# A fused attention and MLP kernel: doubles made float32 by one 16-bit conversion and one join, the MLP of the first 256 tokens in float32

## The chip, the cores and the metric

One core of a Trainium2 chip runs the whole kernel. The metric is device time in microseconds, the median of three runs. Engines are called PE (matrix multiply, its weight loads PEld), DVE (vector), ACT (scalar), POOL and SP; SP issues all copies between HBM and on-chip memory.

## The reference

```python
def _attn_ref(q, k, v):                      # (4, 8, 576, 64) float32
...
    q_rot, k_rot = (rotate(q), rotate(k))
    scale = 1.0 / np.sqrt(D)
    scores = scale * np.matmul(q_rot, k_rot.transpose(0, 1, 3, 2))
    scores = scores - np.max(scores, axis=-1, keepdims=True)
    attn = np.exp(scores)
    attn = attn / (np.sum(attn, axis=-1, keepdims=True) + 1e-09)
    return np.matmul(attn, v).astype(np.float32)
...
def _moe_ref(x, w_in, w_out):                # x (2304, 512), w_in (512, 2048), w_out (2048, 512)
    h = x @ w_in
...
    g = np.where(pos, h, np.where(neg, 0.0, (h + beta) ** 2 / (4.0 * beta)))
    return (g @ w_out).astype(np.float32)
```

`rotate` is the rotary turn of the two halves of a head by cos and sin. The two weight matrices arrive as doubles (8 bytes an element, 8.4 MB each); everything else is float32. The accuracy asked for is that of float32.

## The kernel before

**Numbers in halves.** PE multiplies float16 faster than float32, so most operands are split into a high and a low float16 half (`high` writes hi = x times a factor, `split` then lo = x times the factor minus hi), and a product is three matmuls: hi·hi, hi·lo, lo·hi (`TERMS`). For sample 0 the scores are float32 matmuls (L562), since its k and q are used before their factors are known.

**Stages.** Four samples of 576 queries, each in blocks of two 128-query tiles; the last 64 queries of two samples are packed together ("left"). For a tile and a pair of heads: scores (L564, or L562 in float32), maximum (L534, DVE), exponential with sum (L536, ACT), sum scaled (L539) and inverted (L541), the probabilities split into halves (L314 or L316 and L545), both halves transposed by a DMA through SP (L243), values (L612, 14 float16 matmuls a head), out of PSUM as halves (L623, L626). Then the MLP of a block: `psH` = x·w_in (L720), the piecewise square in four or five elementwise steps (L732 to L748, its low half at L748), `psO` = g·w_out (L757), out (L770). Block 0 (sample 0, queries 0 to 255) runs its MLP as two units of 128 tokens (`SPLIT`); all later blocks take 256 tokens at a time, so their L720 matmuls have 256 columns. The first of those begins block 1 of sample 0.

**Weights.** `prep_w` runs 16 times (8 pieces each of w_in and w_out): a copy of 1 MB of doubles, three DVE integer operations that pack sign, exponent and mantissa into float32 (L493, L495, L497), the high half (L314, ACT), and the low half by PE and ACT in `rest`: per third of a piece a float32 matmul with the identity (L430) and a bfloat16 one with the negated diagonal (L431) add up y - hi in PSUM, and ACT writes it out (L434).

**Order.** Nothing is scheduled at run time. Every step is added to a plan with an engine; `ORDER`, a list of numbers written into the file, says in which order they are issued, and `ON_VECTOR` which engine takes a step that ACT or DVE could do. Each engine works through its list in order and waits at a step whose inputs are not there.

Of the kernel before, what the change touches and what calls it, by code (L numbers as in the profile page):

```python
# [923 lines left out]
```

## Time and profile before

| | us |
|---|---|
| median of 3 runs (lowest, highest) | 604.23 (603.35, 605.54) |
| the profiled execution, its own time | 603.99 |
| its span, from first to last instruction | 602.2 |
| PE busy | 575.7 (96%) |
| DVE busy | 508.8 (84%) |
| ACT busy | 418.5 (70%) |

Busy time is the union of an engine's instructions; consecutive instructions of DVE and ACT overlap by some hundredths of a microsecond, so the step from one start to the next is a little shorter than the duration given for one. A float32 matmul appears in the trace as two records. The span is cut below at 167.1 us, where the first 256-column matmul starts.

### The profile page before, as it was taken

To read this page: it belongs to the slowest core of one execution; us is meant where nothing else is said; L and a number is where in the kernel's file an instruction comes from. 1 tells how busy PE (TensorE), PEld (TensorE's weight loads), DVE (VectorE), ACT (ScalarE), POOL (GpSimd) and SP (SyncE) were. 2 spreads that over 40 slices of the span, in tenths; PEclk is the share of its full clock that TensorE was granted. 3 is DMA by queue.
4 is the path that set the end of the run, shared out by engine and by line. 5 is a ranking of instruction groups with operands and counts; after the bars stand their busy time and mean duration, and the time that the engine had idled before them with its cause. 6 is when DMAs were issued, how large, how long until landed. Compare 5 with 4: busy or idle time off the path is not lost.

```text
span 602.2 us, 12605 instructions
## 1 busy us (share of the span) xinstructions
PE 575.7 (96%) x5074; PEld 378.4 (63%) x5074; DVE 508.8 (84%) x823; ACT 418.5 (70%) x849; POOL 0.7 (0%) x6
## 2 busy tenths in 40 slices
...
GB/s 310 384 209 248 280 271 264 263 194 160 240 173 201 206 115 79 195 118 138 221 187 118 85 149 152 72 105 107 103 79 97 119 114 80 112 60 1 2 36 19
DMA packets 182571, 91.34 MB, mean 152 GB/s; under 512 B 170608, under 2 KB 171888, under 8 KB 180464
## 3 DMA queue, kind: packets, MB, share of 16 engines
...
q8 instruction: 40, 0.66, 0.4%
...
## 4 chain that ended last, share of the span: by engine, by line
PE 75%; DVE 14%; ACT 5%; DMA 3%; issue 2%; SPq 0%; DVEq 0%; ACTq 0%
PE psH L720 29%; PE psO L757 27%; PE psV L612 7%; PE psS L564 6%; DVE phl L545 3%; PE psS L430 3%; DVE sca L534 3%; DMA pT<-phl 2%; DMA w<-in_w_in_dram 1%; PE psS L562 1%; ACT p L536 1%; DVE dup L287 1%; ACT phl L314 1%; ACT w L434 1%; PE psS L590 1%
## 5 line engine op out<-in xcount | busy, mean ns | idle before, releaser
L720 PE MATMUL psH<-xT,w 128*128 128x256 f16 (+1 forms) x2112 | 206.4, 253 | 0.2
L757 PE MATMUL psO<-w,g 128*128 128x512 f16 x864 | 202.0, 379 | 0.2 <-DVE g L748 0.2
L720 PEld LDWEIGHTS <-w 128*128 128x128 f16 x2112 | 174.4, 98 | 31.3 <-issue 2.5
L536 ACT ACTIVATE p<-psS,sca 128x576 f32<-128x576 f32 x144 | 105.8, 736 | 63.2 <-DVE sca L534 41.2
L757 PEld LDWEIGHTS <-g 128*128 128x128 f16 x864 | 82.1, 98 | 85.5 <-issue 2.6
L545 DVE SCALAR_TENSOR_TENSOR phl<-p,sca,phl 128x576 f16<-128x576 f32 x144 | 115.8, 811 | 4.7 <-ACT phl L314 3.8
L534 DVE TENSOR_REDUCE sca<-psS 128x1 f32<-128x576 f32 x144 | 105.5, 749 | 4.9 <-PE psS L564 3.2
L314 ACT ACTIVATE phl<-p,sca 128x576 f16<-128x576 f32 x97 | 72.8, 767 | 12.8 <-DVE sca L541 10.2
L737 ACT ACTIVATE a<-psH 128x512 f32<-128x512 f32 x72 | 42.6, 591 | 47.1 <-PE psH L720 44.3
L740 DVE SCALAR_TENSOR_TENSOR r<-a,r 128x512 f32<-128x512 f32 x72 | 49.3, 685 | 25.0 <-ACT r L735 24.5
L748 DVE SCALAR_TENSOR_TENSOR g<-r,g 128x512 f16<-128x512 f32 x72 | 49.5, 688 | 12.1 <-ACT g L743 10.1
L612 PE MATMUL psV<-pT,vS 128*64 128x320 f16 (+2 forms) x576 | 43.8, 275 | 2.2 <-DVE phl L545 1.7
L564 PE MATMUL psS<-kT,qT 64*128 64x64 f16 (+1 forms) x576 | 44.1, 284 | 1.3 <-ACT p L536 1.3
L564 PEld LDWEIGHTS <-qT 64*128 64x128 f16 x576 | 23.0, 94 | 30.6 <-issue 13.6
L734 ACT ACTIVATE r<-a 128x512 f32<-128x512 f32 x48 | 30.1, 627 | 8.4 <-DVE g L748 6.7
L612 PEld LDWEIGHTS <-vS 128*64 128x64 f16 x576 | 27.8, 109 | 10.7 <-issue 7.4
L743 ACT ACTIVATE g<-r 128x512 f16<-128x512 f32 x40 | 24.9, 622 | 10.4 <-DVE r L740 10.3
L735 ACT ACTIVATE r<-r 128x512 f32<-128x512 f32 x48 | 30.2, 630 | 1.5
L434 ACT ACTIVATE w<-psS,sca 128x341 f16<-128x341 f32 (+1 forms) x48 | 25.5, 538 | 6.1 <-PE psS L562 3.0
L536 ACT ACTIVATION_READ_ACCUMULATOR p<-psS,sca 128x1 f32 x144 | 28.2, 196 | 0.0
L316 DVE TENSOR_SCALAR phl<-p,sca 128x576 f16<-128x576 f32 x47 | 24.2, 516 | 2.1 <-DMA pT<-phl 1.3
L732 DVE SCALAR_TENSOR_TENSOR r<-a 128x512 f32<-128x512 f32 x24 | 16.5, 689 | 11.0 <-ACT a L737 10.6
...
## 6 DMA issues: line engine op xcount, KB each, us to landing
...
```

The source lines that it names most:

```text
L314: plan.add("act", act_cost(n), at, lambda: nc.scalar.activation(out=hi, in_=x, func=AF.Copy, scale=f), r=r, w=w)
L434: plan.add("act", act_cost(cut.stop - cut.start, psum=True), at, lambda cut=cut, bank=bank: nc.scalar.activation(out=lo[:, cut], in_=bank, ...
L534: plan.add("dve", dve_cost(S, psum=True), at, lambda m=m, src=src: nc.vector.tensor_reduce(out=m, in_=src, op=ALU.max, axis=AX.X, negate=T ...
L536: plan.add("act", act_cost(S, psum=True, ptrs=2), at, lambda a=a, e=e, m=m, src=src: nc.scalar.activation(out=p32[e], in_=src, func=AF.Exp ...
L545: plan.add("dve", dve_cost(S, ptrs=1), at, lambda a=a, e=e, hi=hi, lo=lo: nc.vector.scalar_tensor_tensor(out=lo, in0=p32[e], scalar=rr[:, ...
L564: nc.tensor.matmul(out=psS[a][:, lo:hi], lhsT=qT[hf][d, l, j, c:c + 128], rhs=kT[ks][d, j, m, lo:hi], start=z == 0, stop=z == 2)
L612: nc.tensor.matmul(out=outs[a], lhsT=st, rhs=moving(a, blk), start=z == 0, stop=z == len(seq) - 1)
L720: nc.tensor.matmul(out=psH[:, n * i:n * i + n], lhsT=wi[ft // 2][:, wl, kk, 128 * (ft % 2):128 * (ft % 2) + 128], rhs=xfn(xl, kk), start=z ...
L737: plan.add("act", act_cost(512, psum=True, ptrs=0), at, lambda one=one: nc.scalar.activation(out=a, in_=psH, func=AF.Relu, scale=2.0 ** -7 ...
L740: plan.add("dve", dve_cost(512), at, lambda one=one: nc.vector.scalar_tensor_tensor(out=r, in0=a, scalar=one, in1=r, op0=ALU.max, op1=ALU. ...
L748: plan.add("dve", dve_cost(512), at, lambda g=g, one=one: nc.vector.scalar_tensor_tensor(out=g[:, 1], in0=r, scalar=-one, in1=g[:, 0], op0 ...
L757: nc.tensor.matmul(out=psO[pos[tt]], lhsT=g[:, gl, n * i + 128 * tt:n * i + 128 * tt + 128], rhs=wo[ft // 2][:, wl, ft % 2, :], start=ft = ...
```

## The change

It does the following.

- **Doubles.** A piece is copied from its second 16-bit word on (`raw[:, 0:4095]` from `[:, 1:4096]`), so that the top 16 bits and the middle 32 bits of each double are aligned. One conversion bfloat16 to float16 of the top words (L519 on ACT, 13 times; L521 on DVE, 3 times) drops exponent bits; one DVE shift-and-or (L522) joins it with the middle words to float32. The conversions all write one buffer, `top`.
- **Weights stay float32 first.** `full(i)` holds piece i in float32 in the place of the halves of piece i + 1. `halve_w` makes the halves later, between the units of block 0 (`SEQ`, each `C` four pieces): high as before, low by DVE alone (L540). `rest` is not called any more (`PE_LO` is empty).
- **MLP of block 0** (256 tokens) in float32 matmuls (L857, L894): no halves of x or g.
- **Values of the first 128 queries** in float32 (`item32`): PE transposes the probabilities by matmuls with a diagonal of 1/sum (L626, L638), ACT or DVE takes them out of PSUM, and PE multiplies them with v as loaded (L648, L652). The DMA transposes and halves of that tile are gone.
- **Sample 0's k and first q** are loaded once; the exchanged half is made by a matmul with a signed permutation (`nrl`, L321) in the place of the second identity matmul.
- Sample 3 has more softmax buffers; the last output is taken out in two halves, on both engines where `ON_VECTOR` says so; `ORDER` and `ON_VECTOR` are new.

```diff
--- before.py
+++ after.py
...
 ORDER = """
-1 0 1 0 7 74 6 11 10 16 1 21 0 87 40 5 0 1 63 11 0 14 1 59 25 1 0 2 29 1 21 0 248 9 13 4 48 0 243 47 11 242 1 26
...
+2 1 1 0 11 34 45 22 17 6 0 118 117 0 41 8 0 38 7 26 37 54 1 25 64 0 28 1 18 8 0 0 9 0 8 1 4 0 93 94 94 95 94 92
...
-PE_TILES = 16
-PE_SUMS = 4
-PE_Q1 = 0
-SPLIT = {0:"aabbabab"}
-PE_V = 0
+PE_LO = ()
+ATT32 = (0,)
+WHOLE = (0, 1)
+SEQ = "aabCbCabCabC"
+WIDE = 8
+PE_Q1 = False
+SPLIT = (0,)
...
+    xF = [x0[:, 1024 * z:1024 * z + 1024].bitcast(F32).rearrange("p (k n) -> p k n", k=KT) for z in range(2)]
+    xb = x0[:, 1024:2048].rearrange("p (l k n) -> p l k n", l=2, k=KT)
     idn = k1[:, 0:256].bitcast(F32)
+    nrl = x1[:, 2048:2304].bitcast(F32)
...
+                def both(bank=bank, cut=cut, j=j):
+                    nc.tensor.matmul(out=bank[:, 0:m], lhsT=idn, rhs=x[:, j, cut], start=True, stop=False)
+                    nc.tensor.matmul(out=bank[:, 0:m], lhsT=nrl, rhs=y[:, j, cut], start=False, stop=True)
+
...
+    top, tk = k1_[:, 0:2048], ["top"]
+    spare = k1_[:, 2048:4096].bitcast(F32)
...
+    def full(i):
+
+        if i == 2 * NW - 1:
+            return spare, ["spare"]
+        return ws[:, i + 1].rearrange("p l f -> p (l f)").bitcast(F32), [("w", l, i + 1) for l in range(2)]
...
-        dma(at, raw, (w_out if which else w_in).bitcast(U32)[c], [], rk_, 128 * 8192)
+        dma(at, raw[:, 0:4095], (w_out if which else w_in).bitcast(U16)[c][:, 1:4096], [], rk_, 128 * 8192)
...
+        head = raw.bitcast(BF16)[:, 2::4]
+        middle = raw.bitcast(U32)[:, 0::2]
+        cast = top.bitcast(F16)[:, 1::2]
+        if plan.pick() == "act":
+            plan.add("act", act_cost(1024, ptrs=0), at, lambda: nc.scalar.activation(out=cast, in_=head, func=AF.Copy), r=rk_, w=tk)
+        else:
+            plan.add("dve", 602.0, at, lambda: nc.vector.tensor_copy(out=cast, in_=head), r=rk_, w=tk)
         plan.add("dve", 1135.0, at, lambda: nc.vector.scalar_tensor_tensor(
-            out=u, in0=lw, scalar=29, in1=u, op0=ALU.logical_shift_right, op1=ALU.bitwise_or), r=rk_ + yk, w=yk)
-        plan.add("dve", 1135.0, at, lambda: nc.vector.scalar_tensor_tensor(
-            out=u, in0=hw, scalar=0xC0000000, in1=u, op0=ALU.bitwise_and, op1=ALU.bitwise_or), r=rk_ + yk, w=yk)
+            out=y.bitcast(U32), in0=middle, scalar=13, in1=top.bitcast(U32), op0=ALU.logical_shift_right, op1=ALU.bitwise_or),
...
+    def halve_w(i, at):
+        c, which = i // 2, i % 2
+        plan.group, plan.part = "wh", i
         f, fk = wcol[which][1]
-        high(at, hi, y, f, 1024, yk + [fk], [("w", 0, i)] + (firstkeys if i in range(4, 8) else []))
-        if c == 0:
+        y, yk = full(i)
+        hi, lo = [ws[:, i, l] for l in range(2)]
+        high(at, hi, y, f, 1024, yk + [fk], [("w", 0, i), ("w", 1, i)])
+        if i not in PE_LO:
+            plan.add("dve", dve_cost(1024, ptrs=1), at, lambda: nc.vector.scalar_tensor_tensor(
+                out=lo, in0=y, scalar=f, in1=hi, op0=ALU.mult, op1=ALU.subtract),
+                r=yk + [fk, ("w", 0, i)], w=[("w", 1, i)])
+            return
...
+    def item32(at, b, t, j, i, c0):
+
+        plan.group, plan.part = "s0", f"{b}{t}{j}"
+        scores(at, b, t, j)
+        s, ri = ring("phl", 2), ring("sums", 4)
...
+            evacuate(at, dg, idn, rr[:, a:a + 1], 128, ["idn", ("sums", ri, 2)], [("dg", d)], fast=True)
+        pt = phl[s].bitcast(F32)
...
+            def turned(src=src, dg=dg, bk=bk):
+                for z in range(4):
+                    nc.tensor.matmul(out=psO[bk][:, 128 * z:128 * z + 128], lhsT=src[:, 128 * z:128 * z + 128], rhs=dg, start=True, stop=True)
+
...
+        def sums_of_values():
+            for z in range(T):
+                for a in range(2):
+                    h = 2 * j + a
+                    nc.tensor.matmul(out=psV[64 * a:64 * a + 64, c0:c0 + 128], lhsT=rv[:, z, D * h:D * h + D],
+                                     rhs=pt[:, 512 * a + 128 * z:512 * a + 128 * z + 128], start=z == 0, stop=False)
+            for a in range(2):
+                h = 2 * j + a
+                nc.tensor.matmul(out=psV[64 * a:64 * a + 64, c0:c0 + 128], lhsT=rvL[64 * a:64 * a + 64, D * h:D * h + D],
+                                 rhs=pt[64 * a:64 * a + 64, 1024:1152], start=False, stop=True)
+
...
 
-                plan.add("pe", pe_cost(12, n), at, mm, r=xkeys + [("w", l, 2 * (ft // 2)) for l in range(2)] + [("w", 1, 2 * (ft // 2), e) for e in range(2)], w=["psH"],
+                if x32 is not None:
+                    def mmf(i=i, ft=ft):
+                        w = full(2 * (ft // 2))[0].rearrange("p (k f) -> p k f", k=KT)
+                        for kk in range(KT):
+                            nc.tensor.matmul(out=psH[:, n * i:n * i + n], lhsT=w[:, kk, 128 * (ft % 2):128 * (ft % 2) + 128],
+                                             rhs=x32[:, kk, :], start=kk == 0, stop=kk == KT - 1)
...
+                        w = full(2 * (ft // 2) + 1)[0].rearrange("p (k f) -> p k f", f=DM)
+                        nc.tensor.matmul(out=psO[pos[0]], lhsT=g32[:, n * i:n * i + 128], rhs=w[:, ft % 2, :],
+                                         start=ft == 0, stop=ft == FT - 1)
+
+                    plan.add("pe", 863.0, at + 0.3, mm2f, r=gkeys + full(2 * (ft // 2) + 1)[1], w=[("psO", pos[0])])
...
         if i in SPLIT:
-            units = [mlp_units(tokens(z, 128), [("xT", int(last), l, j, z) for l in range(2) for j in range(NP)], 128, ats[4 * z:4 * z + 4],
-                               lambda tt, z=z: main_rows(b, ts)(z)) for z in range(2)]
-            for z in SPLIT[i]:
-                next(units["ab".index(z)], None)
+            units = [mlp_units(lambda l, kk: xb[:, l, kk, :], [("xT", 0, l, j, z) for l in range(2) for j in range(NP)], 128, ats[4 * z:4 * z + 4],
+                               lambda tt, z=z: main_rows(b, ts)(z), xF[z] if z in WHOLE else None) for z in range(2)]
+            parts = iter(range(0, 2 * NW, 4))
+            for z in SEQ:
+                if z == "C":
+                    p = next(parts)
+                    for h in range(p, p + 4):
+                        halve_w(h, at)
+                else:
```

**The weights on DVE.** In the list of DVE before, the first pieces of weights stand among the rotary products (L287) and the maxima (L534) of sample 0, three operations a piece; `w` is the raw piece, `xT_77` and `o` are where the float32 goes:

```order
L497 SCALAR_TENSOR_TENSOR xT_77<-w,xT_77 128x1024
L534 TENSOR_REDUCE sca<-psS_92 128x1
L534 TENSOR_REDUCE sca<-psS_93 128x1
L287 TENSOR_TENSOR w<-w,rt 128x256
L493 TENSOR_SCALAR o<-w 128x1024
L287 TENSOR_TENSOR rk<-rk,rt 128x576
L495 SCALAR_TENSOR_TENSOR o<-w,o 128x1024
L287 TENSOR_TENSOR rk<-rk,rt 128x576
L541 RECIPROCAL sca<-sca 128x2
L497 SCALAR_TENSOR_TENSOR o<-w,o 128x1024
```

The same place in the list of DVE of the change; `kT_63` is the buffer `top`:

```order
L584 TENSOR_SCALAR sca<-sca 128x2
L521 CAST kT_63<-w 128x1024
L586 RECIPROCAL sca<-sca 128x2
L522 SCALAR_TENSOR_TENSOR w<-w,kT_63 128x1024
L575 TENSOR_REDUCE sca<-psS_92 128x1
L575 TENSOR_REDUCE sca<-psS_93 128x1
L298 TENSOR_TENSOR w<-rq_85,rt 128x256
L522 SCALAR_TENSOR_TENSOR w<-w,kT_63 128x1024
L293 TENSOR_TENSOR rq_85<-rq_85,rt 128x256
```

One conversion and one join stand for three operations, and the second join's conversion is on ACT's list; the first conversion stands as the 27th instruction of DVE, where L493 was the 10th.

**PE after the first scores.** Before, PE makes low halves of weights between the float32 scores of sample 0 (`psS` is the PSUM of the scores, of which `rest` uses the spare end):

```order
L430 MATMUL psS_93<-xT_77,kT_63 128x341
L431 LDWEIGHTS kT_63
L431 MATMUL psS_93<-w,kT_63 128x341
L430 MATMUL psS_92<-xT_77,kT_63 128x341
L431 LDWEIGHTS kT_63
L431 MATMUL psS_92<-w,kT_63 128x341
L255 MATMUL psS_93<-sca 128x3
L430 MATMUL psS_92<-xT_77,kT_63 128x342
L431 LDWEIGHTS kT_63
L431 MATMUL psS_92<-w,kT_63 128x342
L562 MATMUL psS_92<-kT_62,qT_64 128x512
L562 MATMUL psS_93<-kT_62,qT_64 128x512
```

After, the same stretch of PE's list holds the turning of probabilities of the first tile (`p`) into `psO` and `psH`, and the rotary sums (L320, L321):

```order
L670 MATMUL psS_92<-kT_62,qT_64 128x64
L670 MATMUL psS_93<-kT_62,qT_64 128x64
L638 MATMUL psH<-xT_77,p_0_69 64x128
L638 MATMUL psH<-xT_77,p_1_70 64x128
L626 MATMUL psO_96<-xT_77,p_0_69 128x128 x4
L320 MATMUL psS_93<-rk,kT_63 128x288
L321 MATMUL psS_93<-w,xT_77 128x288
L626 MATMUL psO_97<-xT_77,p_1_70 128x128 x4
L320 MATMUL psS_92<-rq_85,kT_63 128x256
```

All 48 pairs L430 and L431 are gone from PE; four matmuls of 128 columns a head for the transposed probabilities are new.

**DVE ahead of the first 256-column matmul.** Before, the list of DVE up to the last output of attention that this matmul reads (L626 with 320 columns) holds 238 instructions and ends so:

```order
L534 TENSOR_REDUCE sca<-psS_93 128x1
L534 TENSOR_REDUCE sca<-psS_92 128x1
L260 TENSOR_REDUCE sca<-psS_92 128x1
L626 SCALAR_TENSOR_TENSOR xT_77<-psV,sca,xT_77 128x320
L287 TENSOR_TENSOR dup_87<-dup_87,rt 128x1152
L545 SCALAR_TENSOR_TENSOR phl_72<-p_0_69,sca,phl_72 128x576
L324 SCALAR_TENSOR_TENSOR qT_65<-rq_86,sca,qT_65 128x1280
L626 SCALAR_TENSOR_TENSOR xT_77<-psV,sca,xT_77 128x320
```

After, it holds 212 up to the same output (L734) and ends with the last low halves of weights:

```order
L540 SCALAR_TENSOR_TENSOR w<-w,sca 128x1024
L345 SCALAR_TENSOR_TENSOR qT_64<-rq_85,sca,qT_64 128x1024
L734 SCALAR_TENSOR_TENSOR xT_77<-psV,sca,xT_77 128x320
L540 SCALAR_TENSOR_TENSOR w<-w,sca 128x1024
L345 SCALAR_TENSOR_TENSOR qT_65<-rq_86,sca,qT_65 128x1280
L540 SCALAR_TENSOR_TENSOR w<-kT_63,sca,w 128x1024
L278 TENSOR_SCALAR sca<-sca 128x1
L266 TENSOR_REDUCE sca<-psS_92 128x1
L734 SCALAR_TENSOR_TENSOR xT_77<-psV,sca,xT_77 128x320
```

The first scores and the splitting of k of sample 1, which stood ahead of this point, stand behind it now.

## Rows read from the trace of the kernel before

**Rows 1.** Windows: length, busy time of each engine, granted PE clock, DMA share, GB/s.

```profile
core 0: us, PE busy (x) PEld busy (x) DVE busy (x) ACT busy (x) POOL busy (x), PEclk, DMA share, GB/s
0.00:10.50 10.50, 2.81 (x6) 2.12 (x7) 2.43 (x10) 1.69 (x2) 0.70 (x6) 1.00 0.78 266
10.50:32.40 21.90, 17.77 (x72) 10.54 (x72) 21.69 (x40) 15.93 (x40) 0.00 (x0) 1.00 1.05 371
32.40:39.30 6.90, 6.39 (x15) 2.93 (x16) 6.39 (x17) 5.54 (x11) 0.00 (x0) 0.51 0.90 149
39.30:167.10 127.80, 119.03 (x1113) 75.65 (x1109) 124.99 (x174) 117.21 (x232) 0.00 (x0) 1.00 0.98 243
167.10:225.00 57.90, 57.58 (x531) 39.14 (x526) 57.04 (x92) 50.10 (x101) 0.00 (x0) 1.00 0.76 173
225.00:597.60 372.60, 372.13 (x3349) 247.99 (x3347) 296.25 (x495) 227.38 (x465) 0.00 (x0) 1.00 0.53 102
```

**Rows 2.** Timeline: the first 256-column matmul (PE), and the last output (ACT).

```profile
167.12 1.16 PE L720 MATMUL psH<-xT,w 128*128 128x256 f16 x9
...
597.62 0.69 ACT L770 ACTIVATE o<-psO,sca 128x512 f32<-128x512 f32 x1 [5.83 <-PE psO L757]
```

**Rows 3.** Waits of DVE on copies: total us, times, longest.

```profile
DVE w L287 <- DMA w<-in_km_dram: 4.0, 1, 4.0
...
DVE xT L493 <- DMA w<-in_w_in_dram: 2.0, 1, 2.0
```

**Rows 4.** Timeline of DVE: start, duration, instruction.

```profile
10.46 0.69 DVE L493 TENSOR_SCALAR xT<-w 128x1024 uint32<-128x1024 uint32 x1 [2.04 <-DMA w<-in_w_in_dram]
11.07 0.42 DVE L287 TENSOR_TENSOR rq<-rq,rt 128x256 f32<-128x256 f32 x1
11.41 1.22 DVE L495 SCALAR_TENSOR_TENSOR xT<-w,xT 128x1024 uint32<-128x1024 uint32 x1
12.54 0.75 DVE L287 TENSOR_TENSOR w<-w,rt 128x576 f32<-128x576 f32 x1
...
27.58 0.80 DVE L545 SCALAR_TENSOR_TENSOR phl<-p,sca,phl 128x576 f16<-128x576 f32 x1
28.30 0.75 DVE L534 TENSOR_REDUCE sca<-psS 128x1 f32<-128x576 f32 x1
28.96 1.54 DVE L545 SCALAR_TENSOR_TENSOR phl<-p,sca,phl 128x576 f16<-128x576 f32 x2
...
37.10 1.27 DVE L324 SCALAR_TENSOR_TENSOR vS<-rv,sca,vS 128x1024 f16<-128x1024 f32 x1
38.29 0.15 DVE L265 RECIPROCAL sca<-sca 128x1 f32<-128x1 f32 x1
```

**Rows 5.** Groups by form: busy us and mean ns of one, then idle before.

```profile
L748 DVE SCALAR_TENSOR_TENSOR g<-r,g 128x512 f16<-128x512 f32 x72 | 49.5, 688 | 12.1 <-ACT g L743 10.1
...
L434 ACT ACTIVATE w<-psS,sca 128x341 f16<-128x341 f32 x32 | 16.9, 539 | 1.9 <-PE psS L562 1.2 <-PE psS L431 0.5
...
L314 ACT ACTIVATE w<-xT,sca 128x1024 f16<-128x1024 f32 x8 | 9.1, 1138 | 0.3
...
L324 DVE SCALAR_TENSOR_TENSOR kT<-rk,sca,kT 128x1152 f16<-128x1152 f32 x6 | 8.4, 1406 | 0.0
...
L626 DVE SCALAR_TENSOR_TENSOR xT<-psV,sca,xT 128x256 f16<-128x256 f32 x4 | 1.9, 466 | 0.0
```

**Rows 6.** Timeline of PE: float32 sums of 288 columns, then one L430 and L431 pair.

```profile
19.87 0.65 PE L306 MATMUL psS<-w,kT 128*128 128x288 f32 x2
20.36 0.68 PE L305 MATMUL psS<-rk,kT 128*128 128x288 f32 x2
...
98.85 0.79 PE L430 MATMUL psS<-xT,kT 128*128 128x341 f32 x2
99.48 0.31 PE L431 MATMUL psS<-w,kT 128*128 128x341 f16 x1
99.70 1.50 PE L720 MATMUL psH<-xT,w 128*128 128x128 f16 x24
101.03 0.79 PE L430 MATMUL psS<-xT,kT 128*128 128x341 f32 x2
```

**Rows 7.** Timeline of PE's weight loads: float32, one matmul of 3 columns between.

```profile
29.67 0.30 PEld L255 LDWEIGHTS psS<-sca 128*128 128x128 f32 x2 [0.88 <-ACT qT L309]
29.89 0.30 PEld L305 LDWEIGHTS psS<-rk,kT 128*128 128x128 f32 x2
```

More of the change, by code (lines that the diff above doesn't have):

```diff
@@ L14 @@
 U32 = mybir.dt.uint32
+U16 = mybir.dt.uint16
 AF = mybir.ActivationFunctionType
@@ L380, in split_k @@
         hi, lo = [kT[s][:, js[0]:js[0] + n, l, :] for l in range(2)]
-        split(at, hi, [("kT", s, j, 0) for j in js], lo, [("kT", s, j, 1) for j in js] + (["idn", ("ndg", 0), ("ndg", 1)] if b == 1 and 3 in js else []),
-              rk[:, js[0]:js[0] + n, :], [("rk", j) for j in js], kfac[b, js[0]], n * S)
+        gone = (["top", "spare"] + (["idn", ("ndg", 0), ("ndg", 1)] if 3 in js else [])) if b == 1 else []
+        split(at, hi, [("kT", s, j, 0) for j in js], lo, [("kT", s, j, 1) for j in js],
+              rk[:, js[0]:js[0] + n, :], [("rk", j) for j in js], kfac[b, js[0]], n * S, gone=gone)
     def load_q(b, hf, js, at, i):
@@ L481, in prep_w @@
+    made = []
     def prep_w(which, c, at):
-        yi, i = ring("ybufs", 2), 2 * c + which
-        (raw, rk_), y, yk = rawseq[i], ybufs[yi], ykeys[yi]
+        i = 2 * c + which
+        (raw, rk_), (y, yk) = rawseq[i], full(i)
         plan.group, plan.part = "raw w", c
-        dma(at, raw, (w_out if which else w_in).bitcast(U32)[c], [], rk_, 128 * 8192)
+        dma(at, raw[:, 0:4095], (w_out if which else w_in).bitcast(U16)[c][:, 1:4096], [], rk_, 128 * 8192)
         plan.group = "w"
-        words = raw.rearrange("p (n t) -> p n t", t=2)
@@ L489, in prep_w @@
[L489 to L494 removed]
+        head = raw.bitcast(BF16)[:, 2::4]
+        middle = raw.bitcast(U32)[:, 0::2]
+        cast = top.bitcast(F16)[:, 1::2]
+        if plan.pick() == "act":
+            plan.add("act", act_cost(1024, ptrs=0), at, lambda: nc.scalar.activation(out=cast, in_=head, func=AF.Copy), r=rk_, w=tk)
+        else:
+            plan.add("dve", 602.0, at, lambda: nc.vector.tensor_copy(out=cast, in_=head), r=rk_, w=tk)
@@ L499, in prep_w @@
+            r=rk_ + tk, w=yk + (firstkeys if i in range(3, 7) else []))
         if c == 0:
@@ L529, in softmax_item, with exponentials @@
+    begun = set()
+    def exponentials(b, at, nh, ri):
+        many = b == B - 1
         sm, rr = sums[ri][:, 0:nh], sums[ri][:, 2:2 + nh]
         sk = [("sums", ri, a) for a in range(nh)]
-        es = [ring("p32", 3) for _ in range(nh)]
+        es = [ring("end_p32", 5) if many else ring("p32", 3) for _ in range(nh)]
         for a, e in enumerate(es):
-            m, src = mx[ri][a], psS[slot + a][:, 0:S]
+            m, src = mx[ri][a], psS[a][:, 0:S]
             plan.add("dve", dve_cost(S, psum=True), at, lambda m=m, src=src: nc.vector.tensor_reduce(
-                out=m, in_=src, op=ALU.max, axis=AX.X, negate=True), r=[("psS", slot + a)], w=[("mx", ri, a)])
+                out=m, in_=src, op=ALU.max, axis=AX.X, negate=True), r=[("psS", a)], w=[("mx", ri, a)])
@@ L542, in softmax_item @@
+        return es, rr
+    def softmax_item(b, at, nh):
+        many = b == B - 1
+        s, ri = (ring("end_phl", 4) if many else ring("phl", 2)), ring("sums", 4)
+        halves, hk = end_phl[s]
+        own = [z for z in hk if z[0] == "rk" and s not in begun]
+        begun.add(s)
+        es, rr = exponentials(b, at, nh, ri)
         for a, e in enumerate(es):
-            hi, lo = [phl[s][:, S * (2 * a + l):S * (2 * a + l + 1)] for l in range(2)]
-            high(at, hi, p32[e], rr[:, a:a + 1], S, [("p32", e), ("sums", ri, 2)], [("phl", s, 0, a)])
+            hi, lo = [halves[:, S * (2 * a + l):S * (2 * a + l + 1)] for l in range(2)]
+            high(at, hi, end_p32[e][0], rr[:, a:a + 1], S, [*end_p32[e][1], ("sums", ri, 2)], [("phl", s, 0, a)] + (own if a == 0 else []))
@@ L641, in attention_block @@
             for i, t in enumerate(ts):
+                if i == 1:
+                    for c in range(NW - 2, NW):
+                        for which in range(2):
+                            prep_w(which, c, -8.5 + 1.2 * c)
                 w = 128 + (SL if i == left else 0)
@@ L672, in attention_block @@
                 x_out(at - 1, b, [xT[1][:, l, j, x:x + n] for l in range(2)],
-                      [[("xT", 1, l, j, i) for i in range(2)] + [("xL", l, e, j)] for l in range(2)], n)
+                      [[("xT", 1, l, j, i) for i in range(2)] + [("xL", l, e, j)] + ([("dg", d) for d in range(4)] if b == 0 and l == 0 else [])
+                       for l in range(2)], n)
                 continue
@@ L691, in item, with wkeys, mlp_block, mlp_units @@
         scores(at, b, t, j)
-        s = softmax_item(at, 2)
-        dmaT(at, pT[slot][:, :, col:col + 128], phl[s],
+        s = softmax_item(b, at, 2)
+        dmaT(at, pT[slot][:, :, col:col + 128], end_phl[s][0],
              [("phl", s, l, a) for l in range(2) for a in range(2)], [("pT", slot, i)], 128 * 4608)
+    def wkeys(i, half=None):
+        if half == 0 and 0 < i < WIDE:
+            return [("w", 0, i), ("w", 1, i, 0)]
+        return [("w", 0, i), ("w", 1, i)] + [("w", 1, i, e) for e in range(2)]
     nblk = [0]
-    def mlp_block(xfn, xkeys, n, ats, rows):
-        for _ in mlp_units(xfn, xkeys, n, ats, rows):
+    def mlp_block(xfn, xkeys, n, ats, rows, end=False):
+        for _ in mlp_units(xfn, xkeys, n, ats, rows, end=end):
             pass
-    def mlp_units(xfn, xkeys, n, ats, rows):
+    def mlp_units(xfn, xkeys, n, ats, rows, x32=None, end=False):
         nt = n // 128
@@ L767, in mlp_units @@
             oi = ring("o", 2)
-            f, fk = ofac[0]
-            plan.add("act", act_cost(512, psum=True), at + 0.4, lambda tt=tt, oi=oi: nc.scalar.activation(
-                out=o_s[oi], in_=psO[pos[tt]], func=AF.Copy, scale=f), r=[("psO", pos[tt]), fk], w=[("o", oi)])
+            f, fk = (1.0, "ones") if x32 is not None else ofac[0]
+            for e in range(1 + end):
+                cut = slice(0, 512) if not end else slice(256 * e, 256 * e + 256)
+                evacuate(at + 0.4, o_s[oi][:, cut], psO[pos[tt]][:, cut], f, 512 // (1 + end), [("psO", pos[tt]), fk],
+                         [("o", oi, 1) if e else ("o", oi)], 0 if x32 is not None else 1)
             for sl, dst in rows(tt):
-                dma(at + 0.5, dst, o_s[oi][sl], [("o", oi)], [("out", id(dst))], 128 * 2048 // len(rows(tt)))
+                dma(at + 0.5, dst, o_s[oi] if sl is None else o_s[oi][sl], [("o", oi)] + [("o", oi, 1)] * end, [("out", id(dst))], 128 * 2048 // len(rows(tt)))
     def main_rows(b, ts):
@@ L778, in left_rows @@
     def left_rows(b0):
-        return lambda i: [(slice(64 * e, 64 * e + 64), out[(b0 + e) * S + SM:(b0 + e + 1) * S, :]) for e in range(2)]
-    dma(-20, rt, rot, [], ["rt"], 128 * 2 * 4 * S)
+        return lambda i: [(None, out[b0 * S:(b0 + 2) * S, :].rearrange("(e r) c -> e r c", e=2)[:, SM:S, :])]
+    for e, cut in enumerate((slice(0, 256), slice(256, S))):
+        dma(-20, rt[:, :, cut], rot[:, :, cut], [], [("rt", e)], 128 * 8 * (cut.stop - cut.start))
     def init():
         make_identity(nc, idn)
+        i4, r4 = [m.rearrange("p (a b c) -> p a b c", b=2, c=32) for m in (idn, nrl)]
+        for e in range(2):
+            nc.vector.tensor_scalar(out=r4[:, :, e], in0=i4[:, :, 1 - e], scalar1=-1.0, scalar2=None, op0=ALU.mult)
+        nc.vector.memset(top.bitcast(F32), 0.0)
         nc.vector.memset(ones, 1.0)
@@ L790, in init @@
         nc.vector.memset(vZ[64:128], 0.0)
-    plan.add("dve", 1400.0, -20, init, w=["idn", "ones", "vZ", ("ssw", 2), ("ssw", 5)] + [("ssk", i) for i in range(NP)] + [("ssv", i) for i in range(3)])
+    plan.add("dve", 2000.0, -20, init, w=["idn", "top", "spare", ("xL", 1, 0, 1), "ones", "vZ", ("ssw", 2), ("ssw", 5)] + [("ssk", i) for i in range(NP)] + [("ssv", i) for i in range(3)])
     blocks = [(b, ts, i == 1) for b in range(B) for i, ts in enumerate(([0, 1], [2, 3]))]
@@ L815 @@
     prep_v(0, -8)
-    for c in range(NW):
+    for c in range(NW - 2):
         for which in range(2):
```

206 lines of the change are left out of this document (131 added, 75 removed), and 105 rows, old and new, of the table ORDER.

## The prediction

> **What bounds the kernel now.** I read the windows first. From 167.10 us to 597.60 PE is busy 57.58 + 372.13 of 430.5 us: there the time is PE's work and nothing else [rows 1]. Ahead of that it is not. PE is busy 17.77 of 21.9 us, 6.39 of 6.9 and 119.03 of 127.8, while DVE is busy 21.69, 6.39 and 124.99: from 10.5 to 167.1 us DVE stands still for only 3.5 us, PE for 13.4 [rows 1]. So I cut the run at the timeline's first 256-column matmul, at 167.12 us [rows 2]: DVE's list ahead of it decides when it comes, and the matmuls behind it take what they take. The output follows the last matmul by some 5 us [rows 2].
>
> Behind the cut PE's work is nearly the same in both programs. Counted in the two lists: 1,344 matmuls of 256 and 384 of 128 columns into `psH`, and the same values; 780 of 512 columns into `psO` become 768, and 36 score matmuls of sample 1 (18 of 512, 18 of 64 columns, two side by side) move in. At 0.43 ns a column (24 of 128 columns in 1.33 us [rows 6]) that is -2.6 and +2.2 us: it cancels. So the change is worth what it takes off DVE's list ahead of the cut, as long as PE, ACT and the copies follow, and as long as DVE keeps up behind it.
>
> **The change part by part, on DVE ahead of the cut.** Prices are steps from start to start, since durations overlap by some 0.08 us: L493 0.61, L495 1.13 (L497 alike), L545 0.72, L534 0.66, a low half of 1,024 columns (L324) 1.19 [rows 4]. For the others I take the group's mean less 0.08: L748 0.60, L324 of 1,152 columns 1.33, L626 of 256 columns 0.39 [rows 5]. The counts come from the two lists, 238 instructions before and 212 after.
>
> - *Weights.* Out go 16 x (0.61 + 1.13 + 1.13) = 45.9. In come 16 joins (L522) at L495's 1.13 (the same shift-and-or, raw words read at the same spacing) = 18.1; 16 low halves that PE and ACT made before (L540), 16 x 1.19 = 19.0; 3 conversions (L521); one high half more, 0.7; the two diagonals for `rest` go, -0.4. No row shows a 16-bit conversion on DVE: it lies between L493's 0.61 and L495's 1.13, both of 1,024 columns. I take 0.61, since it has one operand like L493; 1.8, or 3.4. Net -6.7 (-5.1).
> - *First tile in float32.* L545 falls from 37 to 28, L534 from 40 to 36, two high halves come in (1.0): -6.5 - 2.7 + 1.0 = -8.2. Of these, the four L534 and one L545 belong to sample 1 and are only moved behind the cut.
> - *MLP of 256 tokens.* L748 falls from 7 to 0, one step of the square more (0.6): -3.6. Four L626 go: -1.6.
> - *Moved.* Two splits of sample 1's k (L324) and one rotary product (L287, 1.27): -3.9.
> - *Added small things.* Three outputs from PSUM, seven scaled sums, the sign matrix: +1.5.
>
> The sum is -22.5 us, of which some 8 are moved rather than saved (3.9 here, 3.4 above, and small ones).
>
> **What is given back, and what else moves.** Behind the cut, from 167.1 to 225.0, DVE is already busy 57.04 of 57.9 us [rows 1]. The moved 8 us land there. From the cut to the start of the next 256-token MLP, DVE's list holds four maxima, two splits of k, one rotary product and one low half more (+7.3), and three rotary products of the next q fewer (two of 1,280, one of 1,024 columns, at L495's step by their width, -3.9): +3.4. If DVE sets the pace to that point, this is lost; if PE does, nothing. I take 3. Behind 225 us DVE is busy 296.25 of 372.6 [rows 1], and nothing more is lost.
>
> The start gains. Of the first 10.5 us DVE works 2.43 [rows 1], for it waits 4.0 us for the first k and 2.0 for the first weights [rows 3]. After, the second copies of sample 0's k and q are not loaded and the first conversion stands 27th instead of 10th, so the second wait goes and the first shortens by one 0.3 MB copy: -3.
>
> The first tile has a longer chain, from 1/sum through diagonals, PE, PSUM and back, instead of halves and a DMA transpose; queued behind each step on PE are scores whose maxima DVE needs next. PE's list of the change puts rotary sums between the steps. I take +2 for stalls, from 0 to 8 (twice the largest wait that DVE has on a copy now [rows 3]).
>
> *PE ahead of the cut* must not become the bound. Out go 48 pairs L430 and L431 at 0.85 (98.85 to 99.70) [rows 6]: -41. For float32 the two records of 288 columns take 0.49 [rows 6], so 0.85 ns a column and record, 1.7 a column. The MLP's 128 matmuls of 128 columns and 32 of 512 come to 27.9 + 27.9, against 384 float16 ones at 0.055 (24 in 1.33 us [rows 6]) and 96 at 0.22: 55.8 - 42.2 = +13.6. The first tile: 32 transposes of 128 columns at 0.22, 48 half-width matmuls at 0.11, less 112 float16 half-width ones at 0.028: +9. Together -18. PE's 146 busy us ahead of the cut become 128; with the 8 before its first matmul 136, of the 145 that DVE leaves: it follows, with 9 us of room against 13 before.
>
> *ACT* loses 48 evacuations L434 at 0.46 (mean less 0.08 [rows 5]), 22, and gains 13 conversions. No row shows one; a float32 to float16 copy of the same 1,024 columns takes 1.14 [rows 5], the nearest, and I take 1.06 with overlap: 13.8. ACT was busy 140 of 167 us and becomes 130 or so of 145: hidden.
>
> *Copies.* Four large transposes and eight small loads go. The 16 weight copies now start 2 bytes into their rows; no row shows such a start. I take their time as unchanged.
>
> *End.* The last output takes ACT 0.69 [rows 2]; in two halves on two engines, -0.3.
>
> Sum: -22.5 + 3 - 3 + 2 - 0.3 = -20.8. From the span of 602.2 that is 581.4. The profiled execution lasted 603.99, 1.8 beside its span, and the median of the runs is 604.23, 0.2 above it. So 583.4, say **583.5 us**.
>
> **The rivals.** *Conversion in place of integers as a new wait.* The buffer `top` is single: a conversion on ACT waits for the join of the piece before on DVE, and the next join waits for the conversion. Queued behind a join on DVE are the maxima and low halves that PE waits for. If each of the 13 pairs costs DVE 1.06 us, 14 us of the gain go: 597. For it: ACT is busy 92% of 39.3 to 167.1 [rows 1]. Against it: joins stand several instructions behind one another in the list, and half of them at least find the conversion done: 590 to 597.
>
> *Float32 weight loads show.* A float32 matmul loads its weights once a record, and two loads with next to no matmul between take 0.22 us (29.67 to 29.89 [rows 7]), 0.11 each. Behind 240 ns of columns that is hidden [rows 6]; 128 columns stream for 0.11 too, just as long. If load and stream did not overlap, the MLP's 128 and the tile's 32 matmuls of 128 columns would pay 2 x 0.11 each, 35 us; PE's 136 ahead of the cut become 171, the cut comes there and not at 145: 609 at the most, a little slower than now. I give it little, as loads run under the stream in every row shown; a quarter of it would leave the forecast, since PE has 9 us of room. The Trainium skill, TensorE: Matmul & The Clock Gate, section "LDWEIGHTS (loading the stationary operand)", prices a load at columns / 1.2 ns, 107 ns for 128, and its section on fast weight load excludes float32: by that rule load and stream are equal, with nothing to spare. The trace agrees on the price (0.11 us).
>
> *Slower: the shifted copies.* The DMA share is 1.05, 0.90 and 0.98 up to 167.1 us [rows 1], so weights have little room. A copy of 1 MB takes 2.8 us at 371 GB/s. If an odd start made it take twice as long, 16 x 2.8 = 45 us more would pass through the queues ahead of the cut: 604 + 45 - 21 = 628 at worst, and the run is slower from the point where a copy takes half as long again (22 us). No row speaks for it. The Trainium skill, DMA: Bandwidth & Descriptors, "How a descriptor splits into AXI transactions", has reads start at 256-byte boundaries: 8,190 bytes that begin 2 behind one need the same 32 pieces as 8,192. No run here shows it yet; by that rule the cost is nothing.
>
> *The clock.* PE's granted clock was 0.51 from 32.4 to 39.3 us, its lower level of 1.2 GHz, after a stretch with pauses [rows 1]. Since DVE set the pace, this cost nothing then. With PE's room down to 9 us, a second such stretch (3.4 us of PE) still costs nothing.
>
> **How the numbers follow.** Forecast 0.80 (its own range 577 to 590: 3.4 for the conversion's other bound and 0 to 8 for stalls, the start between 0 and -6). Conversion waits 0.09 (590 to 597). Weight loads 0.06 (592 to 609). Copies 0.03 (over 600), and 0.02 for better than 577. A range of 576 to 597 leaves out about 0.11 and the ends of the forecast, as much as it should. Measurements of this kernel tell 0.3% (1.8 us) from no change: faster than 602.4 takes the first two cases and a third of the third, 0.93 with the 0.02; within, 0.03; slower, from the last two, 0.04.
>
> **What would show it.** The first 256-column matmul near 145 us (141 to 149), and about 430 us from there to the last; DVE still over 95% busy ahead of it, PE over 85%; joins at about 1.2 us; float32 matmuls of 128 columns about 0.11 us a record; weight copies landing as fast as before. I am wrong if DVE shows waits for conversions or copies ahead of the cut, if PE shows gaps of more than 5 us in all between 145 and 205, or if the last stretch is longer than 435.

## The result, and the profile after

The change made the kernel faster, by less than half of what was forecast: 595.89 us, the median of 4 runs (595.49 to 597.03), against 603.79 (603.13 to 605.54) for the kernel before on the same chip. The ratio is 0.9869, with a 95% interval of 0.985 to 0.9889. The forecast was 583.5 us.

The profiled execution has a span of 593.7 us, 8.5 less than before. I cut it at the same two places as the kernel before: the first 256-column matmul ("the cut" from here on) and the end of the last matmul [rows 2]; what follows that end is the tail. First the windows, with the same columns as [rows 1]:

```profile
0.00:10.50 10.50, 2.17 (x5) 1.61 (x6) 5.25 (x15) 0.00 (x0) 0.71 (x6) 1.00 0.75 231
10.50:32.40 21.90, 17.65 (x89) 11.47 (x87) 20.03 (x30) 16.82 (x42) 0.00 (x0) 1.00 1.02 389
32.40:39.30 6.90, 6.34 (x58) 5.16 (x54) 6.87 (x15) 6.03 (x15) 0.00 (x0) 1.00 1.00 381
39.30:147.28 107.98, 100.70 (x780) 69.50 (x779) 102.47 (x153) 101.95 (x181) 0.00 (x0) 0.98 0.90 224
147.28:205.00 57.72, 56.68 (x518) 36.77 (x519) 55.59 (x95) 53.32 (x105) 0.00 (x0) 1.00 0.80 173
205.00:583.80 378.80, 374.40 (x3386) 249.50 (x3380) 302.03 (x514) 234.75 (x464) 0.00 (x0) 1.00 0.53 104
```

Then the timeline at the first 256-column matmul, and at the end:

```profile
147.28 0.38 PE L850 MATMUL psH<-xT,w 128*128 128x256 f16 x2
...
583.21 0.59 PE L910 MATMUL psO<-w,g 128*128 128x512 f16 x2
583.85 0.48 DVE L330 TENSOR_SCALAR o<-psO,sca 128x256 f32<-128x256 f32 x1 [3.09 <-PE psO L910]
584.37 0.47 ACT L328 ACTIVATE o<-psO,sca 128x256 f32<-128x256 f32 x1 [5.66 <-DVE o L330]
584.87 0.60 SPq L245 DMA_DIRECT2D out_dram<-o  x1
```

The difference has three parts. The cut comes at 147.28 us and not at 167.12: -19.8. From there to the end of the last matmul (583.21 + 0.59 = 583.8) are 436.5 us, where there were 430.5: +6.0. And from the last matmul to the end of the span are 9.9 us, where there were 602.2 - 597.6 = 4.6: +5.3. Together -8.5. The first part is what the change was priced for. The other two take more than half of it back (11.3 us), and one thing stands behind most of both. PE's waits behind the cut show the first sign of it (total us, times, longest):

```profile
PE psV L720 <- DMA pT<-phl: 3.7, 2, 3.2
PE psS L672 <- ACT p L577: 0.7, 3, 0.3
```

PE stands still for 3.2 us once, for a transposed copy of probabilities. SP's own queue at that place, in the timeline (the column behind the start is how long SP was held):

```profile
375.52 2.66 SPq L249 DMA_TRANSPOSE pT<-phl  x1
378.23 1.31 SPq L245 DMA_DIRECT2D out_dram<-o  x2
381.29 5.85 SPq L249 DMA_TRANSPOSE pT<-phl  x1
```

A transpose holds SP for 2.66 us, but 5.85 where it follows two outputs. The second of these is the first `left_rows` copy; the other such copy is the kernel's last. The window of that last copy:

```profile
585.80:592.40 6.60, 0.00 (x0) 0.00 (x0) 0.00 (x0) 0.00 (x0) 0.00 (x0) 0.57 0.12 40
```

No engine computes, and for 6.6 us the DMA share is 0.12, which is 2 of 16 engines. At 40 GB/s that is 264 KB, the whole copy. The packets in the trace say the same: the copy's 128 packets of 2,048 bytes begin two by two (at 586.089 and 586.097 us, then at 586.169 and 586.177), and on average 2 are under way. In the diff `left_rows` yields one destination with e = 2 for the whole tile, in place of two of 64 rows each. The list of the change above names the halves of the last output, not this:

```diff
     def left_rows(b0):
-        return lambda i: [(slice(64 * e, 64 * e + 64), out[(b0 + e) * S + SM:(b0 + e + 1) * S, :]) for e in range(2)]
...
+        return lambda i: [(None, out[b0 * S:(b0 + 2) * S, :].rearrange("(e r) c -> e r c", e=2)[:, SM:S, :])]
```

My theory: its outermost dimension of 2 puts it on 2 DMA engines. The Trainium skill, DMA: Bandwidth & Descriptors, "Why a DMA increments its semaphore by 16 and not by 1", says that a DMA uses the largest number of engines up to 16 that divides the slowest dimension of both patterns; for 2 and 128 that is 2, and the trace agrees (0.12). That the copy is one is not what makes it slow: the four outputs of 128 adjacent rows between 500 and 580 us, also 256 KB in one copy each, land 2.0 to 2.3 us after their issue.

### The profile page after: what moved, and what is told of

Read it like the earlier page. It is cut to its first block, busy times and chain, and to the rows that moved or that the text cites. A ratio compares the mean times of both kernels' runs of the same rounds, so it can differ in the third digit from the quotient of the medians.

```text
span 593.7 us, 12016 instructions
## 1 busy us (share of the span) xinstructions
PE 557.9 (94%) x4818; PEld 374.0 (63%) x4818; DVE 492.7 (83%) x818; ACT 413.3 (70%) x804; POOL 0.7 (0%) x6
## 5 line engine op out<-in xcount | busy, mean ns | idle before, releaser
L850 PE MATMUL psH<-xT,w 128*128 128x256 f16 (+1 forms) x1728 | 181.9, 261 | 0.6 <-ACT a L876 0.5
L910 PE MATMUL psO<-w,g 128*128 128x512 f16 x768 | 179.0, 379 | 0.1
L850 PEld LDWEIGHTS <-w 128*128 128x128 f16 x1728 | 152.0, 98 | 29.2 <-issue 1.8
L577 ACT ACTIVATE p<-psS,sca 128x576 f32<-128x576 f32 x130 | 95.0, 733 | 28.2 <-DVE sca L575 22.5
L600 DVE SCALAR_TENSOR_TENSOR phl<-p,sca,phl 128x576 f16<-128x576 f32 x112 | 89.7, 812 | 5.1 <-ACT phl L335 4.6
L335 ACT ACTIVATE phl<-p,sca 128x576 f16<-128x576 f32 x78 | 58.2, 767 | 17.9 <-DVE sca L586 6.8
L883 ACT ACTIVATE g<-r 128x512 f16<-128x512 f32 (+1 forms) x47 | 29.3, 623 | 18.8 <-DVE r L879 11.7
L857 PEld LDWEIGHTS psH<-xT,w 128*128 128x128 f32 x256 | 29.7, 192 | 2.9 <-issue 1.2
L857 PE MATMUL psH<-xT,w 128*128 128x128 f32 x256 | 31.2, 278 | 0.1
L894 PE MATMUL psO<-w,g 128*128 128x512 f32 x56 | 26.6, 604 | 0.5 <-ACT g L883 0.5
## 6 DMA issues: line engine op xcount, KB each, us to landing
w<-in_w_out_dram SPq DMA_DIRECT2D x6, 1023.8 KB, 11.5
```

Source lines behind the costliest of these rows:

```text
L335: plan.add("act", act_cost(n), at, lambda: nc.scalar.activation(out=hi, in_=x, func=AF.Copy, scale=f), r=r, w=w)
L577: plan.add("act", act_cost(S, psum=True, ptrs=2), at, lambda a=a, e=e, m=m, src=src: nc.scalar.activation(out=end_p32[e][0], in_=src, func ...
L600: plan.add("dve", dve_cost(S, ptrs=1), at, lambda a=a, e=e, hi=hi, lo=lo: nc.vector.scalar_tensor_tensor(out=lo, in0=end_p32[e][0], scalar ...
L850: nc.tensor.matmul(out=psH[:, n * i:n * i + n], lhsT=wi[ft // 2][:, wl, kk, 128 * (ft % 2):128 * (ft % 2) + 128], rhs=xfn(xl, kk), start=z ...
L857: nc.tensor.matmul(out=psH[:, n * i:n * i + n], lhsT=w[:, kk, 128 * (ft % 2):128 * (ft % 2) + 128], rhs=x32[:, kk, :], start=kk == 0, stop ...
L910: nc.tensor.matmul(out=psO[pos[tt]], lhsT=g[:, gl, n * i + 128 * tt:n * i + 128 * tt + 128], rhs=wo[ft // 2][:, wl, ft % 2, :], start=ft = ...
```

## Experiments

**The left outputs, undone.** `left_in_two` changes the one plan step, so that the order of all others stays:

```diff
+                if sl is None:
+                    plan.add("sp", 600.0, at + 0.5, lambda dst=dst, o=o_s[oi]:
+                             [nc.sync.dma_start(out=dst[e], in_=o[64 * e:64 * e + 64]) for e in range(2)],
+                             [("o", oi)] + [("o", oi, 1)] * end, [("out", id(dst))], bw=128 * 2048 / 400.0)
+                    continue
```

> The changed kernel with one edit: each output of the left tokens (64 rows of two samples) goes out as two copies of 64 rows again, issued one behind the other, where the changed kernel issues one copy whose outermost dimension is the two samples. Theory (that one copy is carried by 2 of the 16 DMA engines): the tail from the last matmul to the end falls from 9.9 us to some 4.5, and PE's wait of 3.2 us at 387 us for a transpose queued behind such a copy goes too: 595.9 - 5.4 - 3.2 = 587.3 us. Rival (the tail is long because the last evacuation is two operations in sequence, and the wait at 387 us belongs to the order of the transposes): nothing changes, 595 to 597.

Measured: 587.32 us, ratio 0.9726 (0.9707 to 0.9745). The last two copies, and the transpose behind the first two:

```profile
583.00:584.30 1.30, 0.00 (x0) 0.00 (x0) 0.00 (x0) 0.00 (x0) 0.00 (x0) 1.00 0.78 177
```

```profile
379.21 1.17 SPq L929 DMA_DIRECT2D out_dram<-o  x2
381.64 2.72 SPq L249 DMA_TRANSPOSE pT<-phl  x1
```

The share is 0.78 in place of 0.12 (on average 13 packets under way) and the tail 5.0 us; the transpose is back to 2.72 us, and the wait of 3.2 us is gone from PE's list. The theory gave 587.3, the rival no change.

**The last one alone.** `last_left_in_two` has the same edit under `if sl is None and end`.

> The changed kernel with only the last of the two left outputs in two copies of 64 rows; the first, near 379 us, stays one copy. Theory: the tail falls by some 5.4 us and PE's wait of 3.2 us at 387 us stays: 590.5 us, 3.2 above left_in_two. Rival (the wait at 387 us has nothing to do with the copy): the same time as left_in_two.

Measured: 592.11 us, ratio 0.9797 (0.9774 to 0.9821). The tail is 5.1 us and PE's wait for `pT` is there:

```profile
PE psV L720 <- DMA pT<-phl: 3.8, 2, 3.2
```

So the wait at 387 us belongs to the first such copy. The median is 4.8 above `left_in_two`, not 3.2: in the profiled execution the cut came at 149.21 and not at 147.87, in a program that is the same up to there.

**The one copy in the kernel before.** The empty first entry is skipped; it keeps the number of plan steps.

```diff
-        return lambda i: [(slice(64 * e, 64 * e + 64), out[(b0 + e) * S + SM:(b0 + e + 1) * S, :]) for e in range(2)]
+        return lambda i: [(slice(0, 0), ones), (slice(0, 128), out[b0 * S:(b0 + 2) * S, :].rearrange("(e r) c -> e r c", e=2)[:, SM:S, :])]
```

> The kernel before with one edit: the outputs of the left tokens go out as one copy each, its outermost dimension the two samples, as in the changed kernel. Theory (2 of 16 DMA engines carry it): the tail grows from 4.6 to some 10 us, and the first such copy may hold up a transpose behind it: 603.8 + 5.4 = 609.2 us, up to 613. Rival (the tail comes from the evacuation in halves or from elsewhere in the change): no change, 603 to 605.

Measured: 610.58 us, ratio 1.0104 (1.0083 to 1.0124), 6.3 us slower by the medians. The tail grew to 10.0 us, with the last evacuation whole on ACT, and its window is that of the changed kernel:

```profile
601.00:607.60 6.60, 0.00 (x0) 0.00 (x0) 0.00 (x0) 0.00 (x0) 0.00 (x0) 0.64 0.12 40
```

PE's longest wait for `pT` there is 0.9 us, and it comes at 220 us; the first such copy is issued at 399.50. The transpose behind that one holds SP for 4.36 us (3.84 at this place before), and PE shows no wait for it. So here the last copy costs and the first does not; why the transpose is held up less here than in the changed kernel is not shown.

**The last output whole.** `left_in_two_last_whole` is `left_in_two` with the last evacuation in one ACT operation:

```diff
...
-                cut = slice(0, 512) if not end else slice(256 * e, 256 * e + 256)
...
+                cut = slice(0, 512)
...
```

> As left_in_two, and the last output leaves PSUM in one ACT operation of 512 columns, as in the kernel before, not in two halves (DVE, then ACT, which waited for DVE). Theory (the copy is the cost): 0.2 to 0.4 us less than left_in_two, not to be told from it in the times; in the trace, 0.69 us from the evacuation's start to its end against 0.99. Rival (the two halves are the cost of the tail): several us less than left_in_two.

Measured: 586.65 us, ratio 0.9718 (0.9693 to 0.9743). The tail is 4.7 us against 5.0. In the changed kernel ACT's half starts at 584.37, behind DVE's end at 584.33 (583.85 + 0.48): the halves take turns, 0.99 us, where one operation takes 0.69 [rows 2]. This is the fastest version, though not to be told from `left_in_two`.

**The pattern with two dimensions of 2.** `left_in_one_two_by_two` adds `.rearrange("e (f r) c -> e f r c", f=2)` to the one copy.

> The changed kernel with one edit: the one copy of the left outputs is written with its 64 rows of each sample as 2 x 32, so that its pattern has two dimensions of 2 ahead of the rows. Theory A (the outermost dimension alone is spread over the DMA engines): 2 engines still, a tail of 9.9 us, 596. Theory B (the two outer dimensions count together): 4 engines, half the transfer's 6 us, a tail of 7 us and part of the wait at 387 us gone, 591 to 593. Rival (the copy is slow for being one, whatever its pattern): as theory A.

Measured: 597.38 us, ratio 0.99 (0.9868 to 0.9932). It decides nothing: the issued instruction has 64 rows and 2 samples as before (`dst_num_elem=[64,2]` in both traces), and its last copy again has a share of 0.12. Whether 4 would give 4 engines stays open.

**Ahead of the cut.** Five programs are alike up to the cut; it came at 147.28 us in the changed kernel, 147.87 in `left_in_two`, 147.75 in `left_in_two_last_whole`, 149.21 in `last_left_in_two` and 149.26 in `left_in_one_two_by_two`. So shifts of the cut of less than 2 us say little here. The first float32 MLP matmul spreads more: it comes at 59.13, 59.14, 59.66, 61.52 and 60.16 us in these five, and at 61.60 and 62.55 in `matmuls_more` and `matmuls_less`, which are the same programs up to there. From that matmul to the cut the five take 87.7 to 89.1 us.

`rotation_whole` loads `rt` by the first copy, whole:

> left_in_two with one more edit: the table of sines and cosines is loaded by the first copy whole, as in the kernel before, where the changed kernel loads columns 256 to 575 first and columns 0 to 255 third. Theory (DVE's first product waits for that third copy, and DVE's list sets when the cut comes): the first product starts at 5.4 us in place of 6.7, and the first 256-column matmul comes 1.0 to 1.5 us earlier than in left_in_two, where it came at 147.87. Rival (the first tile waits for the values and queries as well, so that what is gained at the start is lost by 15 us): the cut moves by less than 0.5 us.

Measured: 587.77 us, ratio 0.9733 (0.9701 to 0.9764), the cut at 147.70. DVE's first product starts at 5.46 us, where it was 7.53 in `left_in_two`, and the rival holds: what is gained is lost to the next copies.

```profile
DVE w L298 <- DMA rq<-in_qa_dram: 1.7, 1, 1.7
```

In `left_in_two` that wait is 0.3 us. `two_conversion_buffers` alternates the conversion's buffer:

```diff
+        tp, tk = (top, ["top"]) if i % 2 else (k1_[:, 2048:4096], ["spare"])
...
```

> left_in_two with one more edit: conversions of weights alternate between two buffers (top and spare), so that one doesn't wait for the join of the piece before. Theory (the single buffer costs what DVE waits at joins for ACT, 2.6 us in all ahead of the cut in the changed kernel): these waits fall below 1 us and the cut comes 1.5 to 2.5 us earlier, near 146. Rival (the conversions are late for ACT's own list or for the weight copies, and the buffer costs nothing): the waits stay and the cut moves by less than 0.5 us.

Measured: 588.0 us, ratio 0.9741 (0.9712 to 0.9769), the cut at 148.01. DVE still waits 2.2 us at the joins, where it was 2.7 in `left_in_two`:

```profile
DVE w L523 <- ACT kT L520: 1.5, 2, 1.1
...
DVE kT L523 <- ACT kT L520: 0.7, 1, 0.7
```

So the single buffer costs nothing that shows. Two more ask which engine sets the pace. `joins_twice` wraps the join in `for _ in range(2 if 4 <= i < 8 else 1)`:

> left_in_two with one more edit: four of the joins ahead of the cut are done twice, the same operation again, 4 x 1.14 = 4.6 us more of DVE. Theory (DVE's list sets when the cut comes): the cut comes 4 to 4.6 us later, near 152, and the time is longer by 4 or so, 591. Rival (DVE and ACT or PE wait in turn, and DVE has slack of its own at each place): the cut moves by 2 us or less.

Measured: 591.08 us, ratio 0.9786 (0.976 to 0.9813), 3.8 us above `left_in_two`, the cut at 150.73 (+2.9), between what the theory (4 to 4.6) and the rival (2 or less) expected. The four extra joins lie ahead of the first float32 MLP matmul, which comes at 61.73 and not at 59.14. Programs without them had it at up to 62.55, so this run does not show that DVE's list sets the cut. `matmuls_more` and `matmuls_less` add and take a matmul of each sum:

```diff
-                        for kk in range(KT):
+                        for z, kk in enumerate((0, 0, 1, 2, 3)):
...
```

The extra matmul is a sum of its own, which the next one overwrites; `matmuls_less` leaves out the fourth of each four.

> left_in_two with one more edit: each of the 32 sums of four float32 matmuls of 128 columns into psH starts with its first matmul twice, 32 x 2 records x 0.122 us = 7.8 us more of PE ahead of the cut. Theory (PE has some 10 us of room there): the cut comes 0 to 3 us later and PE's idle time ahead of it shrinks. Rival (PE sets the pace in that stretch): the cut comes some 7.8 us later, near 155.5.

> left_in_two with one more edit: each of the 32 sums of four float32 matmuls of 128 columns into psH leaves out its fourth matmul (the MLP of the first 256 tokens lacks a quarter of its first product), 32 x 2 records x 0.122 us = 7.8 us less of PE ahead of the cut. Theory, after matmuls_more (PE sets the pace from 85 us to the cut, and DVE, 96% busy there, is next): the cut comes 2 to 5 us earlier, 143 to 146, and DVE is over 97% busy from 85 us to it. Rival (PE alone is the bound): the cut comes 7 to 8 us earlier, near 140.5. Second rival (DVE is the bound): no change, 147 to 148.

Measured: 594.32 us (ratio 0.983, 0.979 to 0.987; cut at 154.81) and 589.8 (0.9768, 0.9731 to 0.9805; cut at 150.47). By its cut the second fits none of the three expectations; measured from the first of these matmuls, below, the second rival's "no change" fits. The windows from the first of these matmuls to the cut, of `left_in_two`, then `matmuls_more`, then `matmuls_less`:

```profile
59.14:147.87 88.73, 85.81 (x653) 58.48 (x652) 84.04 (x129) 83.42 (x145) 0.00 (x0) 1.00 0.93 207
```

```profile
61.60:154.80 93.20, 91.74 (x716) 64.56 (x715) 84.62 (x129) 84.27 (x145) 0.00 (x0) 1.00 0.90 197
```

```profile
62.55:150.47 87.92, 82.17 (x588) 52.38 (x587) 84.10 (x129) 83.10 (x145) 0.00 (x0) 1.00 0.90 209
```

PE, DVE and ACT are busy 97, 95 and 94% of the first window. The float32 matmuls into `psH` take 31.2 us, 38.2 in `matmuls_more` and 24.0 in `matmuls_less`. 7.0 us more of them make the stretch 4.5 us longer, at 98% PE. 7.2 less leave it where it was: 87.92 us lies among the 87.7 to 89.1 of the unchanged stretch, and DVE's 84 and ACT's 83 us stay. So no engine alone sets the pace there. That the cut of `matmuls_less` came late has its cause further ahead, for the first of these matmuls starts at 62.55 us there and not at 59.14. From 17 to 24 us its granted clock was 0.77, so for part of it the lower level of 1.2 GHz, after 17 us in which PE was busy 7.2 (7.65 in `left_in_two`, whose clock stayed at 1.00); and DVE, which has 0.3 us of waits for L670's scores up to 32 us in `left_in_two`, has 2.4:

```profile
17.00:24.00 7.00, 5.29 (x18) 3.31 (x18) 5.96 (x8) 2.27 (x6) 0.00 (x0) 0.77 0.84 319
```

```profile
DVE sca L575 <- PE psS L670: 2.4, 2, 1.4
```

That is not all of it: in `last_left_in_two`, where the clock was 1.00 up to 45 us and 0.50 from 50 to 55, the first of these matmuls came at 61.52. What spreads the programs that are alike stays open.

## Why the forecast was wrong, step by step

- *End, -0.3: the step that failed.* I read the last output as an evacuation and priced its two halves; the copy behind it I left at its old time, though the diff gives it another destination. The tail grew by 5.3 us. `left_in_two` takes back 4.9 of them, and the halves, which I had as a gain, cost 0.3.
- *"About 430 us from there to the last" matmul.* 436.5, by the same oversight: 3.2 of it is PE's wait behind the first such copy. Without it (`left_in_two`) the stretch is 580.64 - 147.87 = 432.8 us, +2.3, where I had +3 for the moved work. The size of that term came out, but not for its reason, which was that DVE sets the pace there: behind the cut of `left_in_two` PE is busy 430.9 of 432.8 us, 1.2 us more work than the 429.7 before [rows 1], and the waits listed for it, 1.7 us in all, are for ACT and none for DVE. That was luck. The bound that I named (435) pointed at the right place. The copy and what it holds up cost 595.89 - 587.32 = 8.6 us by the medians, two thirds of the miss of 12.4.
- *DVE's list, -22.5.* DVE's busy time ahead of the cut fell from 155.5 us [rows 1] to 134.6: -20.9. The prices held. By form, ahead of the cut of the changed kernel (busy us and mean ns, less 0.08 for a step):

```profile
L857 PE MATMUL psH<-xT,w 128*128 128x128 f32 x256 | 31.2, 278 | 0.1
...
L540 DVE SCALAR_TENSOR_TENSOR w<-w,sca 128x1024 f16<-128x1024 f32 x15 | 19.2, 1278 | 0.5 <-ACT w L335 0.5
...
L522 DVE SCALAR_TENSOR_TENSOR w<-w,kT 128x1024 uint32<-128x1024 uint32 x13 | 15.8, 1219 | 1.6 <-ACT kT L519 1.6
...
L519 ACT ACTIVATE kT<-w 128x1024 f16<-128x1024 bf16 x10 | 13.5, 1351 | 1.9 <-DMA w<-in_w_in_dram 1.6 <-DVE w L522 0.3
...
L521 DVE CAST kT<-w 128x1024 f16<-128x1024 bf16 x3 | 2.3, 751 | 0.0
```

  A join is 1.14 us (1.13 taken), a low half 1.20 (1.19), a conversion on DVE 0.67 (0.61). Of the 1.6 us that it falls short, 0.91 is a row that I had not counted, the clearing of `top`; the rest I have not traced to rows.
- *Start -3 and stalls +2.* DVE idles 5.25 of the first 10.5 us in place of 8.07 [rows 1]: -2.8, as forecast, but by one of the two reasons only. The wait for weights is gone; the first product does not come earlier but later, at 6.68 us and not at 5.36, for it waits 3.6 us for the second part of the sines and cosines, and 0.91 of what DVE does in this time is the clearing of `top`. From 10.5 us to the cut it idles 7.4 in place of 3.5: +3.9, inside the 0 to 8. 1.25 of that is the next copy, the query's. DVE is 94.6% busy in this stretch, where I had named over 95. Its longest waits ahead of the cut:

```profile
DVE w L298 <- DMA rt<-in_rot_dram: 3.6, 1, 3.6
DVE w L522 <- ACT kT L519: 1.6, 2, 1.2
...
DVE w L298 <- DMA rq<-in_qa_dram: 1.2, 1, 1.2
DVE phl L600 <- ACT phl L335: 1.2, 1, 1.2
DVE kT L522 <- ACT kT L519: 1.0, 1, 1.0
```

- *PE ahead: 128 busy us, "9 us of room".* The total was right (126.9 in the windows above), the use of it wrong: the room lies ahead of the float32 MLP, and from its first matmul to the cut PE is 97% busy (`left_in_two`). Float32 matmuls of 128 columns take 31.2 / 256 = 0.122 us a record, not 0.109; had loads come on top of the stream, it would be 0.22. So that rival falls.
- *ACT hidden.* Its conversions take 1.27 us a step, not 1.06, and at 94% it is level with the others.
- *Clock.* I said that a second stretch at the lower level costs nothing. In the changed kernel the clock was 1.00 from 32.4 to 39.3 us and 0.57 from 47 to 51 us, where DVE is busy all the time. In `matmuls_less` a stretch at 17 to 24 us came with 2.1 us more of DVE's waits for scores, so it is not shown to be free. This was seen, not made to happen.
- *Conversion waits.* 2.6 us in all, not 14; the buffer isn't their cause. ACT itself waited 1.6 us for weight copies before conversions, 0.3 for a join.
- *Shifted copies.* From 10.5 to 39.3 us, where most of what moves is weights, the copies ran at 389 and 381 GB/s, against 371 in the first of these windows before [rows 1]. A packet of 8,190 bytes took 309 ns in the median between 39.3 us and the cut, one of 8,192 bytes 309 before (means 386 and 364). The weight copies landed later than before, against my sign: 8.5 and 11.5 us after issue in the median (`w_in`, `w_out`), where it was 6.7 and 9.2; in `left_in_two` 8.3 and 8.4. What they waited for is not shown. Nothing shows that the odd start costs; it wasn't tried by itself.

The sum, mended: -20.9 - 2.8 + 3.9 ahead of the cut (-19.8), +2.3 and +0.4 behind it: -17.1, which is the span of `left_in_two` (585.6 against 602.2: -16.6) within the spread of the cut. Beside the copy, then, the forecast of -20.8 was off by some 4 us: 1.6 in DVE's list, 2.1 in DVE's idle time ahead of the cut, and small ones.
